# The last batch's second product transposed, two of its three column pairs by Strassen's scheme

## The chip, the cores and the metric

The kernel runs on one core of one Trainium2 chip. The metric is the device time of one execution in microseconds (us). A core has five engines with instruction streams of their own: PE (TensorE, matrix products; its weight loads are listed apart as PEld), DVE (VectorE), ACT (ScalarE), POOL (GpSimd) and SP (SyncE, which here only issues transfers). Data lie in DRAM, in the on-chip memory of 128 partitions (SBUF), and in the accumulators of TensorE (PSUM). Transfers are packets on 16 DMA engines, which one queue of SP feeds here; they are taken in the order of issue.

## The reference

Sigmoid attention for 8 batches of 12 heads (448 positions, 64 columns a head), and on its result, as rows of 768, a feed-forward product of 2048 hidden columns.

```python
def _attn_ref(q, k, v):                       # (8, 12, 448, 64)
    scores = q @ k^T / sqrt(64) - log(448)
    return (1 / (1 + exp(-scores))) @ v

def _moe_ref(x, w_in, w_out):                 # x (3584, 768), w_in (768, 2048), w_out (2048, 768)
    h = x @ w_in
    g = h - tanh(h)
    return g @ w_out                          # (3584, 768), float32
```

## The kernel before, in words

The work goes by batches of 448 rows. A batch has attention for six pairs of heads, the *first product* h = x w_in with g = h - tanh(h) as a polynomial behind it, and the *second product* out = g w_out. Each float32 product is made of float16 parts, a high and a low one, as three matmuls: high by high, high by low, low by high. Splitting a value takes one ACT operation (the high part) and one DVE operation (value minus high part). Batch 0 also streams the weights in and converts them; its order of work is a string of letters (`ORDER`), and the program's scheduler sets where its transfers stand in SP's queue. From batch 1 on the order in every engine's stream is that in which the code emits the instructions.

`Builder` is the general program and `Small(Builder)`, a subclass, the path that runs here; the general one stands behind a branch that is not taken.

The first product. Batches 0 to 2 make it classically. From batch `SEVEN` = 3 on it goes by a scheme of Strassen's kind: each of eight pairs of hidden column blocks (k = 0 to 7, each pair holding 256 of the 2048 hidden columns) is made with seven products of half size in place of eight. `seven` emits one, 9 matmuls of 224 columns; a pair has 63. The weights' sums for a pair form a *set* of 1344 KB, kept in DRAM. `fetch(n)` loads a set into one of three slots (`RING`), when `close(k)`, the last two products of the set that had the slot, has been issued. In `Small.moe1` a round of k is `front`, `copy`, `seed`, `cross`, `middle`, `reseed`, `close` (the products and the sums between them in PSUM), then `square`, `times`, `curve`, `value` (the polynomial, on ACT and DVE), and `highs` and `lows` (the split of g). These sets are made in batches 1 and 2 from the converted weights; the transfers `set<-wi` and `set<-unit` (L1267, L1309) store them.

The second product. `moe2` goes over three tiles of 128 tokens. For each it makes both halves of 384 output columns, 16 row tiles of w_out with three matmuls of 384 columns: 288 matmuls (`po`, L921). 64 tokens are left, `por`: 96 matmuls (L969) that fill half of the array each. While the second product of batch b runs, the attention of batch b+1 is done by ACT, DVE and POOL in pieces (`blocks`) between its steps. In the last batch no attention is left, so the second product stands alone, except that `FILL` = 2 of its steps (12 matmuls) are issued ahead of `close(7)`.

Batch 0's weights. w_out comes in 32 pieces `rawo` of 128 x 384 (32-bit words), 16 row tiles for each half of the columns. `conv_load` (L172) issues the load. The conversion turns the raw values into float16 parts in place and ends with `conv_end`. The parts of w_out stay in SBUF in `wo` for the whole program, those of w_in until batch 3 writes its ring over them.

Of the kernel before, what the change touches and what calls it, by code (L numbers as in the profile page):

```python
# [8 lines left out]
F16 = mybir.dt.float16  # L9
# [10 lines left out]
P = 128  # L20
D = 64
# [21 lines left out]
class Builder:  # L43

    KAPPA = KAPPA

    SUMS = 1.0
    NORMS = (3, 5, 7)

# [390 lines left out]
    def defers(self, g):  # L440
        return False

    def split_a(self, a, dve):
# [6 lines left out]
        nc.vector.scalar_tensor_tensor(A[:, 1], a[:, 0], A_SCALE, A[:, 0], op0=ALU.mult, op1=ALU.subtract)  # L450
        return A
# [54 lines left out]
    def stream(self):  # L506
# [120 lines left out]
        for g in range(0, G, 2):  # L627
            h = g + 1
            early = g == 0

            aa = units(g, (0, 1))
            do_av()
            if early:
# [48 lines left out]

            aa = units(h, (2,), lambda: parts_k(g + 3))
            if early:
                do_av()
            keep(h, (2,), aa)
            parts_q(g + 3)
# [102 lines left out]

    def g_scales(self, m):

# [12 lines left out]
        V.tensor_tensor(g2, hb, h3, op=ALU.min)  # L805
        V.tensor_scalar(g2, g2, 2.1, TINY, op0=ALU.mult, op1=ALU.max)
        y = self.pow2(g2, 1, "g")
# [35 lines left out]
    def moe1(self, b, st, splits, ahead):  # L843
# [7 lines left out]
        for k in range(self.NF // 2):  # L851
            ph = self.ps.tile([P, 2, 512], F32, name="ph", tag="sc", bufs=2)
            for e in range(2):
                if e < splits[k]:
                    next(self.rest, None)
                self.product(ph[:, e, :S], self.ks[k], e, xhl)
            g = self.gp.tile([P, 2, 2, S], F16, name="g", tag="g")
            self.gs.append(g)
# [42 lines left out]
    def moe2(self, b, gs):  # L901
# [10 lines left out]

        def store(o, j0, n, cols, queue=nc.sync):
            queue.dma_start(self.out[base + j0 : base + j0 + n, cols], o)

# [66 lines left out]


    def build(self):
        nc, tc = self.nc, self.tc
# [35 lines left out]
    def first(self, weights, early, late):  # L1021
# [13 lines left out]
        def room():  # L1035
            self.stage.release()
            self.gp = self.tc.alloc_tile_pool(name="gp", bufs=self.NF // 2, reuse_waits="tile")

        def mixture():
# [16 lines left out]
            if e:  # L1056
                g = self.gp.tile([P, 2, 2, S], F16, name="g", tag="g")
# [130 lines left out]
class Small(Builder):  # L1188
# [5 lines left out]
    SEVEN = 3  # L1194
    FILL = 2
    RIGHT = {1: 0, 2: 3, 3: 1, 4: 2, 5: 6, 6: 4, 7: 5}
    COPYFIRST = True
# [19 lines left out]
    def __init__(self, ctx, tc, flag, *args):  # L1217
# [13 lines left out]
        self.sets = kept("set", (self.NC // 2, 2, 7, P), F16)  # L1231
        self.raws = kept("raw", (self.NC, 256), F32)
        self.half = self.S // 2
        self.flat = self.wi.rearrange("p a b c -> p (a b c)")
        self.nextx = 0

    def ring(self, n):
# [110 lines left out]
    def high_on_dve(self, g, n, of):  # L1348
        return g >= (self.SEVEN - 1) * self.NP and ((n == 0 and of == 2 and self.HIGHS) or (of == 1 and self.HIGH1))

    def defers(self, g):
# [124 lines left out]
    def moe1(self, b, st, splits, ahead):  # L1476
# [5 lines left out]
        h = self.half  # L1482
        ix, bound = st
        base = (b - self.SEVEN) * self.NB
        self.late = []
# [23 lines left out]
        def copy(k):  # L1509
            copies[k] = c = self.tp.tile([P, 2, h], F32, name="cp", tag="t")  # L1510
            nc.scalar.activation(c[:, 0], banks[k][0][:, h:], AF.Copy)
# [44 lines left out]
        def value(k):  # L1556
            u, m = ms[k]
            V.scalar_tensor_tensor(m, u, C_S, m, op0=ALU.add, op1=ALU.mult)  # L1558

        def tail():  # L1560
# [10 lines left out]

        self.gs = [self.gp.tile([P, 2, 2, self.S], F16, name="g", tag="g") for _ in range(self.NB)]
        for k in range(2):
# [5 lines left out]
        ih, ihk = self.h_scales(ix)  # L1579
        self.Sg, self.iSg = self.g_scales(bound)  # L1580
        for k in range(2):
# [5 lines left out]
        for k in range(1, last):  # L1587
# [6 lines left out]
            seed(k + 1)  # L1594
            value(k - 1)
            close(k)
            square(k)
            times(k)
            m, g = ms[k - 1][1], self.gs[k - 1]
            self.highs(m, g)  # L1600
            cross(k + 1)
            middle(k + 1)
            self.lows(m, g, (0,))
            reseed(k + 1)
            self.lows(m, g, (1,))
            del ms[k - 1]
            if k in self.DEFER and b + 1 < self.B:
# [7 lines left out]
        self.tail = tail()  # L1615

# [81 lines left out]
```

## Time and profile before

| what | value |
|---|---|
| runs | 1139.45, 1138.1, 1138.54 us; median 1138.54 |
| profiled execution | 1139.2 us, span of the instructions 1137.3 us |
| granted TensorE clock | 1.000 of full speed |
| DMA queue of SP | 63696 packets, 147.55 MB, 38.0% of the 16 engines' time |
| last batch, first product | ends with the second product's first steps from 1075.9 us on |
| last batch, second product | 1079.6 to 1132.4 us |

A row of a group reads: line, engine, operation, output <- inputs, shapes, count, then busy us and the mean ns of one, then the idle time ahead of them and what ended it. A row of a timeline has the start in us, the duration in us, and the same names. In a row with "x2" behind it the duration runs from the first one's start to the last one's end. The chain lists, in order of time, the pieces of work that released one another up to the end.

### The profile page before, as it was taken

The numbers are of one execution on the slowest core, as the hardware profiler recorded it, in microseconds if no ns is written. First come the engines' busy times: TensorE is split into PE (matmuls) and PEld (weight loads), VectorE is DVE, ScalarE is ACT, GpSimd is POOL, SyncE is SP. The second block draws the span as 40 slices with busy tenths as digits, with TensorE's granted clock in tenths as the row PEclk, the third lists the DMA queues.
The fourth block names the chain that finished last, engine by engine and source line by source line (L and its number), as shares of the span: only waits on it lengthen the run. The fifth ranks groups of instructions, "written<-read, shape, count | busy, mean of one in ns | idle before, by whom it ended". The sixth has DMA issues, their size and how long they took to land.

```text
span 1137.3 us, 21304 instructions
## 1 busy us (share of the span) xinstructions
PE 1123.9 (99%) x8678; PEld 702.5 (62%) x8678; DVE 807.6 (71%) x1302; ACT 739.7 (65%) x1159; POOL 216.5 (19%) x229
## 2 busy tenths in 40 slices
PE   9999999999999999999999999999999999999998
PEld 2345444555555554569855796559955697559965
DVE  6989699676678787777767686786867777636710
ACT  7987786555886467775676667675676766644610
POOL 0033200014020485310034002320033100330000
PEclk9999999999999999999999999999999999999999
DMA  9992171353222447215622174224622156003301
GB/s 363 404 354 74 29 219 54 83 125 112 75 80 59 141 144 268 73 40 199 236 72 63 51 279 145 63 64 143 246 98 65 43 206 231 17 14 138 128 15 37
DMA packets 64023, 149.28 MB, mean 131 GB/s; under 512 B 18480, under 2 KB 41776, under 8 KB 58800
## 3 DMA queue, kind: packets, MB, share of 16 engines
q1 hardware_dynamic: 63696, 147.55, 38.0%
q8 instruction: 69, 1.13, 0.4%
q10 hardware_dynamic: 224, 0.33, 0.1%
q14 instruction: 34, 0.28, 0.1%
HBM read 119.54 MB, written 28.31 MB: 130 GB/s over the span
## 4 chain that ended last, share of the span: by engine, by line
PE 88%; DMA 4%; DVE 3%; ACT 2%; issue 1%; POOL 1%; SPq 0%; ACTq 0%; DVEq 0%; POOLq 0%
PE po L921 29%; PE ph L1467 16%; PE ph L835 9%; PE acc L463 8%; PE sc L423 8%; PE ph L1047 6%; PE por L969 6%; PE phq L1467 3%; PE php L1467 2%; DMA raw<-moe_w_in 2%; DVE wo L264 1%; ACT a L434 1%; DMA qnn<-q 1%; DVE wi L264 1%; DMA wi<-raw 1%
## 5 line engine op out<-in xcount | busy, mean ns | idle before, releaser
L921 PE MATMUL po<-wo,g 128*128 128x384 f16 x2304 | 389.5, 326 | 1.4 <-DVE g L829 0.7
L921 PEld LDWEIGHTS <-g 128*128 128x128 f16 x2304 | 220.5, 98 | 165.1 <-issue 24.3
L1467 PEld LDWEIGHTS <-wi 128*128 128x128 f16 x2520 | 241.2, 98 | 3.5 <-issue 2.4
L450 DVE SCALAR_TENSOR_TENSOR ahl<-a,ahl 128x896 f16<-128x896 f32 x126 | 156.5, 1254 | 61.7 <-ACT ahl L449 60.3
L434 ACT ACTIVATE a<-sc,nls,rn 128x896 f32<-128x896 f32 x147 | 156.3, 1094 | 50.9 <-PE sc L423 49.5
L1467 PE MATMUL ph<-wi 128*128 128x224 f16 x1890 | 188.5, 259 | 0.1
L494 POOL TENSOR_TENSOR x<-x 128x448 f32<-128x448 f32 x24 | 24.9, 1037 | 488.3 <-ACT x L477 488.3
L835 PE MATMUL ph<-xhl,wi 128*128 128x448 f16 x576 | 109.3, 352 | 0.0
L423 PE MATMUL sc<-Q,K 64*128 64x448 f16 x1008 | 100.8, 353 | 2.4 <-ACT a L434 2.4
L835 PEld LDWEIGHTS <-wi 128*128 128x128 f16 x576 | 56.2, 98 | 52.8 <-issue 0.6
L463 PE MATMUL acc<-ahl,vhl 128*64 128x448 f16 (+1 forms) x864 | 80.6, 356 | 0.0
L449 ACT ACTIVATE ahl<-a 128x896 f16<-128x896 f32 x85 | 79.3, 944 | 0.6
L1047 PE MATMUL ph<-x,wi 128*128 128x448 f32 x192 | 74.5, 541 | 0.0
L423 PEld LDWEIGHTS <-K 64*128 64x128 f16 x1008 | 35.6, 97 | 54.2 <-issue 32.9
L969 PE MATMUL por<-wo,g 128*64 128x384 f16 x768 | 64.9, 327 | 0.0
L463 PEld LDWEIGHTS <-vhl 128*64 128x64 f16 (+1 forms) x864 | 38.4, 108 | 40.2 <-issue 19.8
L1544 ACT ACTIVATE u<-ph,ih 128x896 f32<-128x896 f32 x30 | 30.3, 1009 | 43.7 <-PE ph L1467 43.7
L1047 PEld LDWEIGHTS ph<-x,wi 128*128 128x128 f32 x192 | 35.7, 190 | 33.1 <-issue 31.3
L969 PEld LDWEIGHTS <-g 128*64 128x64 f16 x768 | 42.4, 110 | 22.2 <-issue 4.5
L1458 DVE SCALAR_TENSOR_TENSOR g<-m,Sg,g 128x448 f16<-128x448 f32 x80 | 53.4, 678 | 3.7 <-ACT g L1452 3.7
L958 DVE TENSOR_SCALAR o<-po,iK 128x384 f32<-128x384 f32 x20 | 12.3, 616 | 58.9 <-PE po L921 43.5
L1452 ACT ACTIVATE g<-m,Sg 128x448 f16<-128x448 f32 x80 | 48.9, 660 | 6.9 <-DVE m L1558 5.8
(196 smaller groups left out, 1512.8 us busy)
## 6 DMA issues: line engine op xcount, KB each, us to landing
wi<-set SPq DMA_DIRECT2D x40, 1344.0 KB, 5.9
knn<-k SPq DMA_DIRECT2D x45, 224.0 KB, 2.6
qnn<-q SPq DMA_DIRECT2D x44, 224.0 KB, 2.7
rawo<-moe_w_out SPq DMA_DIRECT2D x22, 384.0 KB, 6.0
out<-o SPq DMA_DIRECT2D x21, 384.0 KB, 2.3
raw<-moe_w_in SPq DMA_DIRECT2D x13, 512.0 KB, 8.1
vn<-v SPq DMA_DIRECT2D x24, 256.0 KB, 3.0
raw<-wi SPq DMA_DIRECT2D x8, 768.0 KB, 8.0
```

The lines of the kernel that those rows point to most:

```text
L423: self.nc.tensor.matmul(ps[i * m : (i + 1) * m, h, : self.S], K[i][r, w, c * P : c * P + m], Q[i][r, x, :], start=(n == 0), stop=(n == len ...
L434: self.nc.scalar.activation(a[:, 0], ps[:, :, : self.S], AF.Sigmoid, bias=self.nls, scale=scale)
L449: nc.scalar.activation(A[:, 0], a[:, 0], AF.Copy, scale=A_SCALE)
L450: nc.vector.scalar_tensor_tensor(A[:, 1], a[:, 0], A_SCALE, A[:, 0], op0=ALU.mult, op1=ALU.subtract)
L463: self.nc.tensor.matmul(acc[i][h * D : (h + 1) * D, : self.S], v[k, w, 2 * QT + h if half else h * QT + c], A[k, x, h], start=(n == 0 and ...
L835: self.nc.tensor.matmul(ph, self.wi[:, self.slot(c, k), part, e * P : (e + 1) * P], xhl[c][:, x, :], start=(i == 0), stop=(i == len(prods) ...
L921: nc.tensor.matmul(po[i][:, :H], gs[f // 2][:, x, f % 2, tk * P : (tk + 1) * P], self.wo[:, i * self.NF + 2 * ks[f // 2] + f % 2, w], star ...
L969: nc.tensor.matmul(po[e * D : (e + 1) * D, :H], gs[f // 2][:, x, f % 2, nm:S], self.wo[:, e * self.NF + 2 * ks[f // 2] + f % 2, w], start= ...
L1047: nc.tensor.matmul(ph[:, e, :S], self.fp32(self.wi, self.slot(c, k))[:, 0, e * P : (e + 1) * P], xs[c], start=(c == 0), stop=(c == self.NC ...
L1452: self.nc.scalar.activation(high, src, AF.Copy, scale=self.Sg)
L1458: self.nc.vector.scalar_tensor_tensor(lows[i], srcs[i], self.Sg, highs[i], op0=ALU.mult, op1=ALU.subtract)
L1467: self.nc.tensor.matmul(out, w[:, c, part, left], self.xblock(c, x, right), start=start and i == 0, stop=i == len(prods) - 1, skip_group_c ...
```

## The change

Only the second product of batch 7 (`ACROSS` = 7) is replaced. It is made transposed: out^T = w_out^T g^T, with blocks of 128 output columns as the rows of a result and the 448 tokens as its columns. The rows of the last batch are written so, and the host puts them back when it gathers the output. The six blocks of 128 columns form three pairs, `PAIRS`. The pairs (0, 1) and (3, 4) are made by seven products of half size, whose weights are sums of w_out's blocks; the pair (2, 5) is made by eight products with the plain blocks. `across2` emits the products and `LAST7` writes out their order. `FILL7` = 4 steps (12 matmuls of 224 columns, the first of them 448) stand ahead of `close(7)` in place of `FILL` = 2.

What it adds besides:

- Batch 0. `conv_end` stores the raw values of the pairs' blocks in eight transfers of 512 KB to DRAM (`late<-wo`), one whenever four pieces of a half are complete.
- Batches 1, 3, 4, 5, 6. Sixteen *units* (`late_units`): two loads of raw blocks, four DVE additions on raw blocks, three of 128 columns and one of 256 (`late_add`), the split into high and low parts on ACT and DVE (`late_split`), two stores to DRAM (`lates<-lp`). `LATE` gives each batch's count in the first and the second product, and `STEPS`, `UNITS1` and `UNITS7` their steps.
- Batch 3. `plain_sets` copies w_out's kept parts of the third pair from SBUF to DRAM, eight transfers `lates<-wo` of 128 x 8 x 128 float16.
- Batch 7, first product. Each g is made in seven blocks of 224 columns, four of them sums or differences. `late_value` puts the polynomial's two halves into separate tiles (one of them `gq`, kept for the third pair), `late_sums` and `late_rest` form the sums on POOL (for k = 7 on DVE), and `late_parts` splits them, in DVE operations of 896 and 672 columns where two of 448 were. `late_fetch` loads the weights of the second product, 512 KB each, while the first product still runs: seven into the place where the other batches keep g, further ones into slots of the ring.
- The end. Each result tile of the third pair is scaled into 224 columns and stored by SP (`whole`), where a DVE operation of 384 columns and two stores, one on SP and one on ACT, stood.

SP's stream in batch 3, between the second product of batch 2 and the loads of the first product's sets. `out` are results, `set` a set in DRAM, `wi` the ring's place; the names with `late` are new. First before, then after:

```order
L914 DMA out<-o 128x768
L914 DMA out<-orem 64x384 x2
L1245 DMA wi<-set_112 128x5376
L1245 DMA wi<-set_113 128x5376
L1245 DMA wi<-set_114 128x5376
L1245 DMA wi<-set_115 128x5376
```

```order
L933 DMA out<-o 128x768
L933 DMA out<-orem 64x384 x2
L1397 DMA lates_135<-wo 128x8x128 x8
L1597 DMA wi<-set_112 128x5376
L1597 DMA wi<-set_113 128x5376
L1340 DMA wo<-late_126 128x2x128 x2
L1597 DMA wi<-set_114 128x5376
```

The eight copies now stand ahead of set 112, the fourth set that the first product of batch 3 uses (set 3 in the text), and the loads of a unit behind set 113.

SP's stream in batch 0, where the last pieces of w_out are loaded (`rawo`) among the loads of the next batch's attention inputs (`vn`, `knn`, `qnn`). First before, then after:

```order
L172 DMA rawo<-moe_w_out 128x384
L357 DMA vn<-v 128x512
L172 DMA rawo<-moe_w_out 128x384 x2
L347 DMA knn<-k 128x448
L172 DMA rawo<-moe_w_out 128x384
L347 DMA qnn<-q 128x448
L357 DMA vn<-v 128x384
L172 DMA rawo<-moe_w_out 128x384 x2
```

```order
L173 DMA rawo<-moe_w_out 128x384
L358 DMA vn<-v 128x512
L1308 DMA late_130<-wo 512x1x256
L173 DMA rawo<-moe_w_out 128x384 x2
L348 DMA knn<-k 128x448
L173 DMA rawo<-moe_w_out 128x384
L348 DMA qnn<-q 128x448
L358 DMA vn<-v 128x384
L173 DMA rawo<-moe_w_out 128x384 x2
```

One of the eight stores now stands ahead of the last five pieces.

DVE's stream in the first product of batch 7, one round (`ph` is PSUM, `cp` a copy of a part of it, `u` and `m` the polynomial's tiles, `gt` the sums; from here on `wo` is also the place of batch 7's g parts, whose home it takes). First before, then after:

```order
L1515 TENSOR_TENSOR ph<-ph,cp 128x224
L1558 SCALAR_TENSOR_TENSOR m<-u,m 128x896
L1550 SCALAR_TENSOR_TENSOR m<-ph,ihk,u 128x896
L1458 SCALAR_TENSOR_TENSOR g<-m,Sg,g 128x448
L1529 TENSOR_TENSOR ph<-cp,ph 128x448
L1458 SCALAR_TENSOR_TENSOR g<-m,Sg,g 128x2x224
```

```order
L1888 TENSOR_TENSOR ph<-ph,cp 128x224
L1455 SCALAR_TENSOR_TENSOR gq<-u,m 128x448
L1455 SCALAR_TENSOR_TENSOR m<-u,m 128x448
L1477 SCALAR_TENSOR_TENSOR wo<-m,Sg,wo 128x896
L1923 SCALAR_TENSOR_TENSOR m<-ph,ihk,u 128x896
L1902 TENSOR_TENSOR ph<-cp,ph 128x448
L1477 SCALAR_TENSOR_TENSOR wo<-gt,Sg,wo 128x672
```

The one operation of `value` became two, and the two splits of 448 became one of 896 ahead of `times` and one of 672 behind `reseed`.

The core of the diff:

```diff
+    PAIRS = ((0, 1), (3, 4), (2, 5))
+    LAST7 = (
+        "e04 T T T e03 e01 e14 e13 e11 e21 e23 m04 m03 m01 m14 m13 m11 m21 m23 l04 l03 c0 l14 l13 c1 Q "
...
+    FILL7 = 4
+    LATE = {1: (3, 0), 3: (1, 3), 4: (0, 3), 5: (0, 3), 6: (0, 3)}
...
+    def conv_end(self, p):
+        super().conv_end(p)
+        kind, r, i, n = p["piece"]
+        if kind == "out" and r % 4 == 3:
+            rows = self.fp32(self.wo, i * self.NF + r - 3, 4).rearrange("p f (b n) -> p f b n", n=P)
+            self.nc.sync.dma_start(self.late_raws[i][r // 4], rows[:, :, :2])
...
+    def late_add(self, u):
+        V = self.nc.vector
+        w = u[1][0]
+        V.tensor_tensor(w[:, 4], w[:, 0], w[:, 3], op=ALU.add)
+        V.tensor_tensor(w[:, 5], w[:, 2], w[:, 0], op=ALU.subtract)
+        V.tensor_tensor(w[:, 6], w[:, 1], w[:, 3], op=ALU.subtract)
+        V.tensor_tensor(w[:, 1:3], w[:, 1:3], w[:, 0:4:3], op=ALU.add)
+    def late_split(self, u):
+        raw, high, low = u[1]
+        self.nc.scalar.activation(high, raw, AF.Copy, scale=self.So)
+        self.nc.vector.scalar_tensor_tensor(low, raw, self.So, high, op0=ALU.mult, op1=ALU.subtract)
...
+    def plain_sets(self):
+        for n in range(4):
+            e, f = n % 2, n // 2
+            for x in range(2):
+                rows = self.wo[:, e * self.NF + f : (e + 1) * self.NF : 2, x, 2 * P :]
+                self.nc.sync.dma_start(self.late_sets[2][:, n, :, x], rows)
...
+    def late_sums(self, m, k, G):
+        h = self.half
+        t = self.tp.tile([P, 3, h], F32, name="gt", tag="t")
+        q, p = self.gq[k], m[:, 1]
+        G.tensor_tensor(t[:, 0], q[:, :h], p[:, h:], op=ALU.subtract)
+        G.tensor_tensor(t[:, 1], q[:, h:], p[:, :h], op=ALU.subtract)
+        G.tensor_tensor(t[:, 2], p[:, :h], p[:, h:], op=ALU.add)
+        return t
...
+            for k in ps:
+                for part, x in ((0, 0), (0, 1), (1, 0)):
+                    nc.tensor.matmul(
+                        p if wide == 2 else o,
+                        w[:, k, part],
+                        self.gq[k][:, x, right] if d == 2 and n > 4 else gs[k][:, x, right : right + wide],
...
+        if b == self.SEVEN:
+            self.plain_sets()
...
             seed(k + 1)
             value(k - 1)
+            m, g = ms[k - 1][1], self.gs[k - 1]
+            if late:
+                rest[k - 1] = m, self.late_sums(m, k - 1, nc.gpsimd), g
+                self.late_rest(m, k - 1, nc.gpsimd)
+                if k > 1:
+                    self.late_parts(*rest[k - 2], (1,))
             close(k)
...
-        self.ahead2 = self.moe2(b, self.gs)
-        for _ in range(self.FILL):
+        self.ahead2 = self.across2(b) if late else self.moe2(b, self.gs)
+        for _ in range(self.FILL7 if late else self.FILL):
             next(self.ahead2)
         close(last)
```

More of the change, by code (lines that the diff above doesn't have):

```diff
@@ L47 @@
     SUMS = 1.0
+    ACROSS = 7
     NORMS = (3, 5, 7)
@@ L1232, in __init__ @@
         self.raws = kept("raw", (self.NC, 256), F32)
+        self.marks = {}
+        self.late_raws = [
+            [self.drp.tile([P, 4, 2, P], F32, name=f"late{e}{i}", tag=f"late{e}{i}") for i in range(4)]
+            for e in range(2)
+        ]
+        self.late_sets = [
+            self.drp.tile([P, n, self.NB, 2, P], F16, name=f"lates{d}", tag=f"lates{d}") for d, n in enumerate((7, 7, 4))
+        ]
         self.half = self.S // 2
@@ new lines, in unit_plan @@
+    def unit_plan(self, b, which):
+        at = sum(sum(self.LATE[c]) for c in self.LATE if c < b) + sum(self.LATE[b][:which])
+        units = list(range(at, at + self.LATE[b][which]))
+        if b < self.SEVEN:
+            return units, ((1 if which else 3, 0),), 6 if which else 4
+        return units, ((0, 0), (1, 3)) if which else ((1, 0),)
+    def plain_sets(self):
[4 more added lines that the diff above has]
+                self.nc.sync.dma_start(self.late_sets[2][:, n, :, x], rows)
@@ new lines, in late_plan, with late_fetch @@
+    def late_plan(self):
+        self.late_at = {}
+        self.late_order = []
+        for b in range(self.ACROSS, self.B):
+            for word in (self.LAST7 if b + 1 == self.B else self.STEADY7).split():
+                if word[0] in "ew":
+                    d, n = int(word[1]), int(word[2])
+                    key = b, d, self.left_of(d, n)
+                    if key not in self.late_order:
+                        self.late_order.append(key)
+    def late_fetch(self, at):
+        if self.late_order:
+            b, d, i = self.late_order.pop(0)
+            self.late_at[b, d, i] = at
+            self.nc.sync.dma_start(self.late_ring(at), self.late_sets[d][:, i])
@@ L1237, in ring, with rows7, mm @@
+    def rows7(self, d):
+        return [slice(r * P, (r + 1) * P) for r in self.PAIRS[d]]
+    def mm(self, name):
+        return self.ps.tile([P, 512], F32, name=name, tag="mm", bufs=2)[:, : self.S]
     def ring(self, n):
@@ L1349, in high_on_dve, with beside, eager @@
         return g >= (self.SEVEN - 1) * self.NP and ((n == 0 and of == 2 and self.HIGHS) or (of == 1 and self.HIGH1))
+    def beside(self, b, k, e):
+        if b in self.LATE:
+            if k == e == 0:
+                if b == min(self.LATE):
+                    self.common_scale()
+                self.made = self.late_units(*self.unit_plan(b, 0))
+            for n in range(self.STEPS1[k]):
+                next(self.made, None)
+    def eager(self, g):
+        return g >= self.ACROSS * self.NP and g % self.NP == 0
     def defers(self, g):
@@ L1483, in moe1 @@
         ix, bound = st
+        late = b >= self.ACROSS
+        rest, fetches = {}, {}
+        if late:
+            if b == self.ACROSS:
+                self.late_plan()
+            fetches = {k: tuple(n for n in (2 * k - 2, 2 * k - 1) if n < 7 and b == self.ACROSS) for k in range(1, self.NB)}
+            if b + 1 == self.B:
+                fetches = {k: n + self.EXTRA7.get(k, ()) for k, n in fetches.items()}
         base = (b - self.SEVEN) * self.NB
@@ L1509, in copy @@
         def copy(k):
-            copies[k] = c = self.tp.tile([P, 2, h], F32, name="cp", tag="t")
+            pool, tag = (self.xp, "x") if late else (self.tp, "t")
+            copies[k] = c = pool.tile([P, 2, h], F32, name="cp", tag=tag)
             nc.scalar.activation(c[:, 0], banks[k][0][:, h:], AF.Copy)
@@ L1570, in tail @@
             self.late.append((ms[last][1], (self.gs[last],)))
-        self.gs = [self.gp.tile([P, 2, 2, self.S], F16, name="g", tag="g") for _ in range(self.NB)]
+        self.gs = [self.late_g(k) if late else self.gall[:, k] for k in range(self.NB)]
         for k in range(2):
@@ L1598, in moe1 @@
             times(k)
-            m, g = ms[k - 1][1], self.gs[k - 1]
-            self.highs(m, g)
+            if not late:
+                self.highs(m, g)
             cross(k + 1)
[L1602 to L1605, printed above, removed]
+            if late:
+                middle(k + 1)
+                reseed(k + 1)
+                if k > 1:
+                    self.late_parts(*rest.pop(k - 2), (0,))
+            else:
+                middle(k + 1)
+                self.lows(m, g, (0,))
+                reseed(k + 1)
+                self.lows(m, g, (1,))
             del ms[k - 1]
+            for n in fetches.get(k, ()):
+                self.late_fetch(n)
+            for n in range(self.STEPS[k]):
+                next(made, None)
             if k in self.DEFER and b + 1 < self.B:
@@ L1610, in moe1 @@
         value(last - 1)
-        self.ahead2 = self.moe2(b, self.gs)
-        for _ in range(self.FILL):
+        if late:
+            m, g = ms[last - 1][1], self.gs[last - 1]
+            rest[last - 1] = m, self.late_sums(m, last - 1, nc.gpsimd), g
+            self.late_rest(m, last - 1, nc.gpsimd)
+            self.late_parts(*rest.pop(last - 2), (0, 1))
+            self.late_parts(*rest[last - 1], (0,))
+        self.ahead2 = self.across2(b) if late else self.moe2(b, self.gs)
+        for _ in range(self.FILL7 if late else self.FILL):
             next(self.ahead2)
         close(last)
-        self.tail = tail()
+        for n in fetches.get(last, ()):
+            self.late_fetch(n)
+        for n in range(self.STEPS[last]):
+            next(made, None)
+        self.tail = late_tail() if late else tail()
     def products(self, b):
```

282 lines of the change are left out of this document (273 added, 9 removed), and 3 rows, old and new, of the table STEADY7.

## The prediction

> **What bounds the kernel now.** I read the page first: the busy shares, then the chain that ended last.
>
> ```profile
> PE 1123.9 (99%) x8678; PEld 702.5 (62%) x8678; DVE 807.6 (71%) x1302; ACT 739.7 (65%) x1159; POOL 216.5 (19%) x229
> ```
>
> ```profile
> PE 88%; DMA 4%; DVE 3%; ACT 2%; issue 1%; POOL 1%; SPq 0%; ACTq 0%; DVEq 0%; POOLq 0%
> ```
>
> TensorE is busy for 1123.9 of 1137.3 us, so time falls only where matmul time falls, and time is lost wherever the new work makes TensorE wait. The windows of the last batch come next (stretch; its length; busy us and count of PE, weight loads, DVE, ACT, POOL; granted clock; DMA share; GB/s), with two other places that I need below:
>
> ```profile
> 1028.00:1079.00 51.00, 50.98 (x525) 49.51 (x520) 33.46 (x59) 26.44 (x44) 0.00 (x0) 1.00 0.39 140
> 1079.00:1132.40 53.40, 53.35 (x379) 32.66 (x376) 6.73 (x12) 6.15 (x9) 0.00 (x0) 1.00 0.06 23
> 165.00:170.00 5.00, 5.00 (x38) 2.29 (x35) 4.31 (x8) 4.68 (x9) 1.14 (x1) 1.00 0.83 233
> 650.00:770.00 120.00, 120.00 (x1062) 82.67 (x1062) 88.30 (x135) 85.89 (x141) 21.66 (x23) 1.00 0.40 137
> ```
>
> In its first product (first row) and its second (second row) the last batch leaves TensorE no gap, at full clock, and in the second product everything else is nearly idle. The end of the chain (start, us, what) prices both products:
>
> ```profile
> 1067.28 8.62 PE ph L1467 x90
> 1075.90 1.95 PE po L921 x12
> 1077.85 1.73 PE ph L1467 x18
> 1079.58 44.85 PE po L921 x276
> 1124.43 7.94 PE por L969 x96
> 1132.37 0.02 issue
> 1132.39 0.62 DVE orem L978
> ```
>
> **1. The matmuls, the gain.** Before: 1.95 + 44.85 + 7.94 = 54.74 us for 288 matmuls of 384 columns and 96 in column halves. After: (7 + 7 + 8) products x 16 row tiles of w_out halved into 8 pairs x 3 parts = 22 x 24 = 528 matmuls of 224 columns, two of them twice as wide. A 224-column matmul of the same kind takes 8.62 / 90 = 0.0958 us; 528 of them and twice 0.093 for the extra width are 50.8 us, a gain of **-4.0 us**. The longer stretch gives 50.98 / 525 = 0.0971, which would make it 51.4 and -3.3; I take the chain's, because it has no 448-wide matmul in it, and keep -3.3 to -4.0.
>
> **2. The end.** The last evacuation is a DVE tile of 384 columns (0.62 us) now; then it is one of 224, about 0.40 (a 224-column row stands in part 5). The two last stores are issued side by side now, one by SP and one by ACT:
>
> ```profile
> 1133.04 0.48 SPq L914 DMA_DIRECT2D out<-orem  x1
> 1133.04 0.56 ACTq L914 DMA_DIRECT2D out<-orem  x1
> ```
>
> After the change both go through SP, the second 0.4 to 0.5 later, unless the first is already out by then. -0.22 + 0.45 = **+0.2** (-0.2 to +0.6).
>
> **3. Batch 3, the plain blocks.** Ahead of the load of set 3 in SP's queue come eight copies of 256 KB from the weights on chip to DRAM, in runs of 256 bytes, 8192 runs in all. The rows: SP's issues and the landing of one set (KB, us), then PE's use of that set; the last two are batch 1, where twelve transfers with the same 256-byte runs were issued, and the queue's packets, MB and share of 16 engines from 238 to 241 us.
>
> ```profile
> 510.34 1.11 SPq L914 DMA_DIRECT2D out<-orem  x2
> 518.53 0.34 SPq L1245 DMA_DIRECT2D wi<-set  x1
> ```
>
> ```profile
> wi<-set SPq DMA_DIRECT2D x1, 1344.0 KB, 5.8
> ```
>
> ```profile
> 524.56 1.89 PE L1467 MATMUL ph<-wi 128*128 128x224 f16 x18
> ```
>
> ```profile
> 234.61 6.15 SPq L1267 DMA_DIRECT2D set<-wi  x12
> ```
>
> ```profile
> q1 hardware_dynamic: 1571, 0.38, 57.0%
> ```
>
> Set 3 is issued at 518.53, when its slot comes free, lands 5.8 later at 524.4, and TensorE starts on it at 524.56: 0.2 us of slack. The copies can start at 511.45. 57% of 3 us on 16 engines is 27.4 us for 1571 packets, 17.4 ns for one; 8192 of them are 8.9 us of all sixteen engines. With some 1.5 us until the first moves (a small store takes 2.3 in all) they occupy the engines until about 522. Set 3 then begins behind them, with 1344 KB to move, and lands near 526.5: **+2.0**. Bounds: +0 if the copies drain before 518.5, +9 if SP's issue is what grows with the number of runs (rival B). Later sets are fetched as slots come free, all later by the same amount, so the loss is paid once. The Trainium skill, "DMA: Bandwidth & Descriptors", section "Anatomy of one DMA — SWDGE (gpsimd) path", fits a transfer as about 2.0 us plus its bytes at 436 GB/s and says that a DMA can emit many descriptors before they add cost; by that the 2.1 MB would be an estimated 6.8 us, over at 518.3, and the sum below would be 2.0 lower. The trace's 256-byte packets moved 0.38 MB in 3 us at a share of 57%, 222 GB/s at a full share, half that rate, so I take the trace.
>
> **4. Batch 0, the raw blocks kept.** Eight DMAs of 512 KB write w_out's columns 0-1 and 3-4 to DRAM while the weights stream in. The fourth (late_130) is ahead of the loads of pieces 11 to 15 in SP's queue. The chain there:
>
> ```profile
> 164.97 1.51 SPq L172
> 166.53 5.42 DMA rawo<-moe_w_out
> 172.24 0.27 issue
> 172.50 1.15 ACT wi L261
> ...
> 208.22 0.59 ACT oh L940
> 208.86 4.06 PE po L921 x24
> ```
>
> The load issued at 164.97 ends the chain's wait, and from it a chain of conversions on ACT and DVE runs to the matmuls at 208.86 without a pause. The queue moves 233 GB/s at a share of 0.83, 281 at a full one: 512 KB cost 0.524 / 281 = 1.87 us of it. With 17% of it free some of that is taken up: **+1.2** (0 to +1.9). The other seven stand at places where the queue's loads are not on this chain; nothing for them, and 1.9 for each that turns out to be.
>
> **5. Batch 7, first product.** Its g parts become seven blocks with sums, so VectorE's round changes. One round of before (start, us, engine, line, op, shapes, idle before):
>
> ```profile
> 1070.29 0.63 DVE L1529 TENSOR_TENSOR ph<-cp,ph 128x448 f32<-128x448 f32 x1 [0.51 <-ACT cp L1525]
> 1070.83 0.68 DVE L1458 SCALAR_TENSOR_TENSOR g<-m,Sg,g 128x448 f16<-128x448 f32 x1
> 1072.02 0.40 DVE L1515 TENSOR_TENSOR ph<-ph,cp 128x224 f32<-128x224 f32 x1 [0.51 <-ACT cp L1511]
> 1072.95 1.09 DVE L1558 SCALAR_TENSOR_TENSOR m<-u,m 128x896 f32<-128x896 f32 x1 [0.53 <-ACT u L1554]
> 1074.40 1.15 DVE L1550 SCALAR_TENSOR_TENSOR m<-ph,ihk,u 128x896 f32<-128x896 f32 x1 [0.36 <-ACT u L1544]
> 1075.46 0.68 DVE L1458 SCALAR_TENSOR_TENSOR g<-m,Sg,g 128x448 f16<-128x448 f32 x1
> ```
>
> That is 4.63 us in a round of 63 matmuls, 63 x 0.0958 = 6.04. The work on SBUF alone grows from 896 + 896 columns (1.09 + 0.68 + 0.68 = 2.45) to 448 + 448 + 896 + 672 = 2464: by the 1.09 row 3.0 us, by the 0.68 row 3.7, so about 3.4 and a round of 5.5. GpSimd gets three sums of 224 columns and one of 448 a round. What that does to VectorE shows where both work now:
>
> ```profile
> 718.50 3.65 DVE L450 SCALAR_TENSOR_TENSOR ahl<-a,ahl 128x896 f16<-128x896 f32 x2
> ```
>
> ```profile
> 719.34 1.87 POOL L503 TENSOR_TENSOR x<-x,x 128x448 f32<-128x448 f32 x1
> ```
>
> ```profile
> L1369 POOL TENSOR_TENSOR wi<-x,x 128x224 f32<-128x224 f32 x15 | 9.8, 655 | 37.1 <-ACT x L477 37.1
> ```
>
> Two VectorE operations of 896 columns took 3.65 us beside GpSimd, against 2 x 1.09: they wait for each other. GpSimd's 3 x 0.655 + 2 x 0.655 = 3.3 us (the 448 counted as two of 224) and VectorE's 3.4 together need 6.6 us of a 6.04 us round. If VectorE's operations on PSUM (2.2 us) can lie beside GpSimd, which no row here tells, the round is 0.6 too long in the worst order, and the slack in it (four waits of 0.36 to 0.53) is used up. At the product's end 18 matmuls (1.73 us, x18 in the chain) close the last block; ahead of them now stand 12 of 384 columns (1.95 us), then 12 of 224 (1.15). 0.8 us of cover goes where seeds are already tight. **+1.0** (0.2 to 3.4, the upper end 6 rounds x 0.56).
>
> **6. Batches 1 and 3 to 6, the 16 sums.** A unit is two loads, four additions, a split on ACT and one on DVE and two stores: by the 1.09 row some 2.2 us of DVE and 1.0 of ACT, three in a batch of 120. In the window 650 to 770 DVE is free for 31.7 us and ACT for 34.1, and TensorE has no gap, so 6.6 and 3.0 us are covered; what is not covered is a unit that stands ahead of an attention piece, up to 1.1 us at a time. **+0.3** (0 to +1.0). Without that cover all 16 would cost 35 us.
>
> **The sum**: -4.0 + 0.2 + 2.0 + 1.2 + 1.0 + 0.3 = +0.7 us. The profiled execution took 1139.2 us with a span of 1137.3, 0.7 over the median of 1138.54 (runs from 1138.1 to 1139.45), so 1139.9 in its terms and **1139.2 us** in the median's. What this measurement can tell from no change is 0.2%, 2.3 us: 1136.3 to 1140.8.
>
> **Rival A, faster.** The copies of part 3 are gone before set 3 is issued: at 281 GB/s, the full-share rate of the window from 165 us, 2.1 MB take 7.5 us, 511.45 to 519, about when set 3 is issued. Batch 0's slack in the queue takes late_130, and GpSimd finds its gaps. Then -4.0 + 0.2 + 0 + 0 + 0.5 + 0.3 = -3.0, **1135.5 us**. For it: TensorE's end is a clean 54.7 us of matmuls, and losses below 1.7 us in all are enough. Against it: 17.4 ns a packet, and 0.2 us of slack.
>
> **Rival B, slower.** SP itself takes long over 1024 runs: the twelve issues with 256 runs took 6.15 / 12 = 0.51 each, that of a set with 128 took 0.34. In proportion to runs eight issues of 1024 are 8 x 4 x 0.51 = 16.4 us, 511.45 to 527.9, and set 3, issued behind them, lands at 533.7: TensorE waits 9.1 us instead of 2.0, **1146.3 us**. It decides from 1.4 us an issue on (set 3 issued at 522.4, a stall of 3.6, a sum of 2.3). Against it: the two 64-run stores took 1.11 / 2 = 0.55 each, so the time of an issue does not follow the runs. By the difference of 0.34 and 0.51 alone, 0.17 for 128 runs, an issue of 1024 would be 1.5 and the stall near 4.7.
>
> **Rival C, slower.** VectorE and GpSimd exclude each other in every round of batch 7 (part 5's upper end): 3.4 instead of 1.0, **1141.6 us**. The four waits for ACT in the quoted round, 1.9 us, speak against it; 3.65 us for two operations speaks for it. The Trainium skill, "SBUF — State Buffer", section "SBUF: two separate sides", has this as an exclusive lock held for a whole instruction by whichever of a VectorE operation with two SBUF inputs and a GpSimd operation starts first; the 3.65 us agrees.
>
> That the change does not do what it says would show as more than 0.097 us a matmul; the 90 in a row of the same shape speak against it.
>
> **How the numbers follow.** The forecast, a stall of some 2 us at set 3 and a net near zero: 0.45. Rival A 0.25, B 0.17, C 0.13. The forecast's own range is 1137.6 to 1140.8. The range to 8 in 10 takes in A and C and leaves out most of B: 1135.3 to 1143.6. Faster by over 0.2%: most of A and a little of the forecast, 0.25. Within: 0.44. Slower: B, most of C and a little of the forecast, 0.31.
>
> **What would show it.** 528 matmuls near 0.096 us each at the end; a gap in PE ahead of its first use of set 3 (about 2 us; none for A, 5 or more with SP busy all the while for B); the conversions after the load of piece 11 about 1 us later against TensorE's first use of them; in batch 7 GpSimd's sums above 0.655 and VectorE's above 1.09 where they meet, and PE waiting for VectorE's seeds there. The prediction is wrong if there is a wait in batches 3 to 6 that I have put at nothing, or if the stores at the end are late.

## The result, and the profile after

The changed kernel takes 1146.29 us (median of 6 runs, 1144.17 to 1148.34), the kernel before 1138.99: ratio 1.0065, 95% interval 1.0052 to 1.0079. It is 7.3 us slower, outside the range. The profiled execution took 1148.34 us, 9.1 more than the one of before; the sums below go by these two, and the six runs of the changed kernel spread over 4 us where those of before spread over 1.5. Why they spread shows below.

The page's busy shares and chain, as shown of before:

```profile
PE 1125.1 (98%) x8822; PEld 720.9 (63%) x8822; DVE 871.3 (76%) x1413; ACT 762.8 (67%) x1186; POOL 249.4 (22%) x257
```

```profile
PE 68%; DVE 8%; DMA 4%; ACT 3%; issue 2%; SPq 1%; POOL 1%; DVEq 0%; POOLq 0%; ACTq 0%
```

TensorE is busy for 1125.1 us in place of 1123.9, though it has about 3 us less to do, and 7.9 us more of the span are idle. So two things are new: waits, and matmuls that take longer. The view of what TensorE waited for (total us, times, longest) names the waits; the list of before has neither the first, the third nor the fourth row:

```profile
PE ph L1831 <- DMA wi<-set: 5.0, 2, 3.7
PE sc L424 <- ACT a L435: 3.8, 4, 1.4
PE ph L850 <- DVE m L2087: 2.3, 1, 2.3
PE po L940 <- DVE o L977: 1.4, 4, 0.4
```

The matmuls up to the last second product are the same in both kernels, one by one, so the start of each can be subtracted from the start of its partner. That lag moves only at these places (us, the profiled executions):

| place | lag gained | of it idle | priced at |
|---|---|---|---|
| batch 0 and on, to 260 us | -0.3 | 0 | +1.2 (part 4) |
| batch 1, first product, 272.6 | +4.1 | 2.3 | in the +0.3 of part 6 |
| batch 2, to 500 us | -0.1 | 0 | 0 |
| batch 3, set 3, 528.4 | +5.2 | 3.7 | +2.0 (part 3) |
| batch 4, its first fetched set, 666.2 | +1.5 | 1.3 | 0 |
| batches 3 to 6, one evacuation each | +2.1 | 1.4 | in the +0.3 of part 6 |
| batch 7, first product | 0 | 0 | +1.0 (part 5) |
| last second product | -3.4 | 0.5 | -4.0 (part 1) |
| the end | 0.0 | | +0.2 (part 2) |

They add up to 9.1. In two places clearly more is lost than the wait. The windows of batch 1 (first three rows) and batch 3 (last four) show it (stretch; length; busy us and count of PE, weight loads, DVE, ACT, POOL; granted clock; DMA share; GB/s):

```profile
272.00:274.90 2.90, 0.62 (x4) 0.20 (x2) 2.59 (x4) 2.45 (x3) 1.04 (x2) 1.00 0.84 239
274.90:278.00 3.10, 3.08 (x10) 1.33 (x10) 3.08 (x3) 2.47 (x3) 3.10 (x3) 0.60 0.79 200
278.00:281.00 3.00, 3.00 (x15) 1.48 (x14) 2.95 (x4) 2.38 (x4) 1.75 (x3) 0.85 0.31 109
526.00:528.40 2.40, 2.40 (x26) 2.22 (x24) 2.11 (x3) 2.04 (x3) 0.00 (x0) 1.00 1.08 299
528.40:532.20 3.80, 0.07 (x1) 0.00 (x0) 2.53 (x4) 1.19 (x2) 0.00 (x0) 0.91 0.98 405
532.20:535.00 2.80, 2.79 (x16) 2.29 (x17) 0.00 (x0) 0.00 (x0) 0.00 (x0) 0.52 0.76 287
535.00:538.00 3.00, 3.00 (x34) 3.00 (x32) 1.58 (x3) 2.39 (x5) 0.00 (x0) 1.00 0.04 13
```

Behind the wait TensorE is busy all the time, but the granted clock is 0.52 to 0.60, and 16 matmuls take 2.8 us where 26 took 2.4. The "busy" column hides that loss. The same view, cut where the granted clock changes, shows where that happens (batch 1, then batch 3):

```profile
272.08:275.50 3.42, 1.12 (x7) 0.49 (x6) 3.11 (x4) 2.96 (x4) 1.64 (x3) 1.00 0.89 262
275.50:278.91 3.41, 3.41 (x11) 1.42 (x10) 3.38 (x4) 2.79 (x4) 3.41 (x3) 0.50 0.54 122
528.08:531.50 3.42, 0.40 (x5) 0.14 (x2) 2.85 (x5) 1.19 (x2) 0.00 (x0) 1.00 0.97 395
531.50:534.91 3.41, 2.70 (x15) 2.21 (x16) 0.00 (x0) 0.00 (x0) 0.00 (x0) 0.50 0.83 326
```

By the traces' record of the granted clock it changes in all ten profiled executions only at whole multiples of 3.41 us from one another; the two halvings above begin 256.0 us apart, 75 such stretches. A full clock was halved behind a stretch in which TensorE was busy for little (33% in the first row, 12% in the third, 37% at most over all executions), and never behind one with 52% or more. So what counts is not the length of a wait alone but how much of one stretch it fills, and half speed then lasts for whole stretches.

SP's stream in batch 3 answers to the rows of part 3 (start, us):

```profile
515.42 8.04 SPq L1397 DMA_DIRECT2D lates<-wo  x8
523.57 2.68 SPq L1597 DMA_DIRECT2D wi<-set  x2
```

The eight copies are issued in 8.04 us, 0.6 to 0.7 us each at first and 1.14 to 1.20 once the engines are full (their share is 1.06 to 1.10 from 518 to 526 us). The load of set 3 is issued at 523.57, where its slot had been free since about 522.2 (518.53 in the kernel before, and a lag of 3.7 by then), and lands 8.6 us later at 532.2, where 5.8 was usual. TensorE's rows:

```profile
527.45 1.03 PE L1831 MATMUL php<-wi 128*128 128x224 f16 x9
532.21 3.20 PE L1831 MATMUL ph<-wi 128*128 128x224 f16 x18 [3.73 <-DMA wi<-set]
535.24 1.89 PE L1831 MATMUL php<-wi 128*128 128x224 f16 x18
```

The middle row's 18 matmuls take 3.20 us, the last row's 1.89: half speed, then full.

In batch 1 the chain shows what was late (start, us, what):

```profile
262.96 0.52 SPq L1363
...
263.58 0.62 SPq L1363
...
264.25 0.74 SPq L1340
...
265.04 5.26 DMA lu<-late
...
270.39 0.29 DVE lu L1347
```

A unit's loads (L1340) are issued from 264.25 on, behind twelve transfers of the sets (in runs of 256 bytes) and the stores of the unit before (L1363), and the second lands 5.26 us after its issue at 265.04. VectorE has stood at the addition (L1347) all that time:

```profile
DVE lu L1347 <- DMA lu<-late: 5.5, 2, 5.3
```

Behind the additions, in VectorE's order, stand a split of the sets, the unit's split and the polynomial (`m`, L2087) that frees the accumulators for TensorE. VectorE was idle for 5.3 us and then everything came at once. The price of a unit was not its 2.2 us of work but the in-order wait for its load.

The evacuations of the second product (L977) were late by half a us once a batch, here in batch 3:

```profile
608.10 1.22 DVE L1347 TENSOR_TENSOR wi<-wi 128x128 f32<-128x128 f32 x1
609.24 0.74 DVE L1348 TENSOR_TENSOR wi<-wi 128x128 f32<-128x128 f32 x1
609.90 0.74 DVE L1349 TENSOR_TENSOR wi<-wi 128x128 f32<-128x128 f32 x1
610.68 0.76 DVE L1350 TENSOR_TENSOR wi<-wi 128x256 f32<-128x256 f32 x1
611.36 0.60 DVE L977 TENSOR_SCALAR o<-po,iK 128x384 f32<-128x384 f32 x1
```

Four additions take 3.3 us just ahead of it, where those of batch 1 took 0.28 to 0.43 each; GpSimd is at its sums of the next batch there, and the operations of the two engines start in turn, some 0.7 us apart on each:

```profile
609.12 0.71 POOL L1733 TENSOR_TENSOR wi<-x,x 128x224 f32<-128x224 f32 x1
609.79 0.70 POOL L1734 TENSOR_TENSOR wi<-x,x 128x224 f32<-128x224 f32 x1
```

The traces of the eight kernels with units hold 128 such groups of four additions. The 20 with GpSimd busy all through took 3.34 to 3.36 us from the first one's start to the last one's end; the other 108 took 1.14 to 1.16, all but one of them with GpSimd idle.

The last batch has neither wait nor slow matmuls. Its first product, with VectorE at 94% and GpSimd at 61%, and its second product:

```profile
1060.00:1090.00 30.00, 30.00 (x315) 29.88 (x313) 28.23 (x37) 21.80 (x33) 18.23 (x20) 1.00 0.89 339
1090.00:1141.00 51.00, 50.91 (x529) 50.38 (x527) 21.95 (x38) 15.00 (x22) 4.89 (x5) 1.00 0.27 96
```

### The profile page after: what moved, and what is told of

The parts are those of the page before. It is cut to its first block, busy times and chain, and to the rows that moved or that the text cites. A ratio compares the mean times of both kernels' runs of the same rounds, so it can differ in the third digit from the quotient of the medians.

```text
span 1146.4 us, 21959 instructions
## 1 busy us (share of the span) xinstructions
PE 1125.1 (98%) x8822; PEld 720.9 (63%) x8822; DVE 871.3 (76%) x1413; ACT 762.8 (67%) x1186; POOL 249.4 (22%) x257
## 3 DMA queue, kind: packets, MB, share of 16 engines
q8 instruction: 70, 1.15, 0.4%
## 4 chain that ended last, share of the span: by engine, by line
PE 68%; DVE 8%; DMA 4%; ACT 3%; issue 2%; SPq 1%; POOL 1%; DVEq 0%; POOLq 0%; ACTq 0%
PE po L940 23%; PE ph L1831 15%; PE acc L470 7%; PE sc L424 7%; PE ph L850 4%; PE por L988 4%; PE phq L1831 3%; PE php L1831 2%; DMA wi<-set 1%; PE poa L1511 1%; DVE wi L265 1%; DMA set<-wi 1%; DMA lu<-late 1%; PE pob L1511 1%; DVE wo L265 1%
## 5 line engine op out<-in xcount | busy, mean ns | idle before, releaser
L940 PE MATMUL po<-wo,g 128*128 128x384 f16 x2016 | 343.0, 326 | 2.8 <-DVE o L977 1.4
L940 PEld LDWEIGHTS <-g 128*128 128x128 f16 x2016 | 192.2, 98 | 148.8 <-issue 26.5
L457 DVE SCALAR_TENSOR_TENSOR ahl<-a,ahl 128x896 f16<-128x896 f32 x126 | 151.9, 1218 | 56.5 <-ACT ahl L456 54.9
L501 POOL TENSOR_TENSOR x<-x 128x448 f32<-128x448 f32 x24 | 27.6, 1152 | 487.1 <-ACT x L484 487.1
L988 PE MATMUL por<-wo,g 128*64 128x384 f16 x672 | 56.9, 327 | 0.0
L1084 PEld LDWEIGHTS ph<-x,wi 128*128 128x128 f32 x192 | 35.8, 190 | 33.1 <-issue 31.7
L1923 DVE SCALAR_TENSOR_TENSOR m<-ph,ihk,u 128x896 f32<-128x896 f32 x30 | 34.5, 1150 | 21.8 <-ACT u L1917 21.8
L988 PEld LDWEIGHTS <-g 128*64 128x64 f16 x672 | 37.1, 110 | 19.5 <-issue 4.2
L510 POOL TENSOR_TENSOR x<-x,x 128x448 f32<-128x448 f32 x21 | 35.7, 1702 | 45.1 <-ACT x L499 43.7
L1822 DVE SCALAR_TENSOR_TENSOR g<-m,Sg,g 128x448 f16<-128x448 f32 x64 | 42.7, 678 | 2.9 <-ACT g L1816 2.9
## 6 DMA issues: line engine op xcount, KB each, us to landing
vn<-v SPq DMA_DIRECT2D x24, 256.0 KB, 3.2
```

Of the source, the lines that this page charges most:

```text
L510: nc.gpsimd.tensor_tensor(out, self.x2, x2, op=ALU.add)
L940: nc.tensor.matmul(po[i][:, :H], gs[f // 2][:, x, f % 2, tk * P : (tk + 1) * P], self.wo[:, i * self.NF + 2 * ks[f // 2] + f % 2, w], star ...
L988: nc.tensor.matmul(po[e * D : (e + 1) * D, :H], gs[f // 2][:, x, f % 2, nm:S], self.wo[:, e * self.NF + 2 * ks[f // 2] + f % 2, w], start= ...
L1084: nc.tensor.matmul(ph[:, e, :S], self.fp32(self.wi, self.slot(c, k))[:, 0, e * P : (e + 1) * P], xs[c], start=(c == 0), stop=(c == self.NC ...
L1822: self.nc.vector.scalar_tensor_tensor(lows[i], srcs[i], self.Sg, highs[i], op0=ALU.mult, op1=ALU.subtract)
```

## The experiments

The theory: the loss has three places, the copies ahead of set 3, the additions in batch 1 that wait for their loads, and the additions ahead of evacuations; with the halved clock after the two long waits. The rival: the 16 units and the 27 MB more of transfers cost time wherever they stand.

**Copies moved.** The copies leave the place ahead of set 3 and are issued two a batch from the events of the second products of batches 3 to 6:

```diff
         if b == self.SEVEN:
-            self.plain_sets()
+            pass
...
+        if self.SEVEN <= b < self.ACROSS:
+            at = 2 * (b - self.SEVEN)
+            events += [(p, lambda i=i: self.plain_set(i)) for i, p in ((at, 13), (at + 1, 44)) if i >= 0]
```

> The changed kernel with the eight copies of the plain blocks taken from their place ahead of set 3 and issued two a batch in the second products of batches 3 to 6. Theory (a wait of 3.7 us for set 3 behind the copies, and about 1.3 us of matmuls at half speed after it): 5 us less than the changed kernel, near 1141.3, and no wait of PE for a set in batch 3. Rival (the copies cost their engine time wherever they stand, since other loads are then late): within 1.5 us of the changed kernel, near 1146, with new waits for loads in batches 3 to 6. Rival (SP's issue is what holds up, 1.2 us a copy): as the theory in time, but the copies' issues in the second products stay at 1.1 us or more each.

Measured: 1140.08 us, ratio to before 1.0007 (0.9998 to 1.0017), 6.2 us less than the changed kernel. No wait for a set is left in batch 3, and none came elsewhere for the copies. The theory's 5 us hold; the rest lies in batch 1, where this profiled execution lost 2.1 us and not 4.1 with the same code. Seven of the copies' eight issues took 0.43 to 0.67 us in their new places and one 1.40, so the second rival does not hold. One wait for a set is there, in batch 4:

```profile
PE ph L1830 <- DMA wi<-set: 1.7, 1, 1.7
```

It is the first set that batch 4 fetches, with 0.2 us of slack. It landed after 7.9 us here, 7.4 in the changed kernel, 7.2 and 7.7 in two more of the ten profiled executions and 5.6 to 5.8 in the other six; nothing else was in the queue. The same load took 5.5 to 5.8 us in batches 5 to 7 of all ten. What makes the one in batch 4 slow these runs don't show.

**Copies alone.** The kernel before with the eight copies at the same place:

```diff
+        if b == self.SEVEN:
+            for n in range(4):
+                e, f = n % 2, n // 2
+                for x in range(2):
+                    rows = self.wo[:, e * self.NF + f : (e + 1) * self.NF : 2, x, 2 * P :]
+                    self.nc.sync.dma_start(self.late_set[:, n, :, x], rows)
```

> The kernel before with the eight copies alone, at the place where the changed kernel has them (written to DRAM and never read). Theory: the copies by themselves make set 3 late, 3.7 us of wait and 1.3 of half speed, 1144 us. Rival (set 3 is late only together with the other work of the change, by my first price): 2 us, 1141.

Measured: 1144.31 us, ratio 1.0052 (1.0037 to 1.0066), 5.2 us over before. The view of TensorE's waits has one new row:

```profile
PE ph L1468 <- DMA wi<-set: 3.5, 1, 3.5
```

So the copies cost their 5 us with nothing else of the change present.

**How many copies fit.** Four, then six, of the eight ahead of set 3, the others in the second products (`i >= 4`, `i >= 6` in the events above, and `for i in range(4)` or `range(6)` where `plain_sets` stood).

> The changed kernel with four of the eight copies left ahead of set 3, the other four in the second products of batches 5 and 6. The copies drained 1.3 us apiece (10.4 us for eight). Theory (what matters is when the engines have drained the copies): four are gone at 521.5, before set 3's slot is free at 521.8, so no wait for set 3, and the time is that of the kernel with all copies later, 1140 us (1139 to 1141.5). Rival (anything in the queue ahead of set 3 makes it late in proportion): half of the loss, 1143.

> The same with six copies ahead. Theory: they drain at 524.1, set 3 lands at 529.5, where TensorE wants it at 528.5: a wait of about 1.0 us. If half speed follows only a longer idle time, as the waits of 0.5 to 0.7 us elsewhere and of 3.7 us here suggest, the loss is 1.0 and the time 1141.1; if half speed follows it too, 1142.3. Rival in proportion: three quarters of the loss, 1144.5.

Measured: 1141.65 us with four, 1141.88 with six, ratios 1.0022 (1.0012 to 1.0031) and 1.0019 (1.0010 to 1.0029). With four there is no wait for set 3 at all; the time is over the 1140 expected, and in the profiled execution batch 1 lost its full 4.2 us:

```profile
PE ph L850 <- DVE m L2090: 2.4, 1, 2.4
```

The granted clock is 0.998 or less in seven of these ten runs, the profiled one among them, and in two of the eleven with all copies later, which speaks for more halvings of the clock here.

With six, set 3 cost 0.5 us of lag (a wait of 0.4), less than the 1.0 expected, and no half speed. So four copies cost 0, six 0.5, eight 3.7 and the clock: not in proportion. From six to eight the engines' work grows by 2.6 us, but set 3 lands 10.0 us after its slot is free in place of 6.5. SP, held at the full queue, issued set 3 only 1.4 us after the slot was free; with six it issued it at once:

```profile
514.43 5.64 SPq L1396 DMA_DIRECT2D lates<-wo  x6
521.28 3.97 SPq L1596 DMA_DIRECT2D wi<-set  x2
```

That late issue left no gap on the engines: with eight copies the last one's packets end at 526.5, and the first packet of set 3 starts at 526.2. The copies end 4.3 us after the slot is free with eight and 2.0 with six. Besides, set 3 lands 5.6 us behind their end with eight and 4.5 with six; why, these runs don't show.

**Units spread in batch 1.** Two units in its first product and one in its second, with six half rounds a unit and the additions three half rounds behind their loads:

```diff
-    LATE = {1: (3, 0), 3: (1, 3), 4: (0, 3), 5: (0, 3), 6: (0, 3)}
+    LATE = {1: (2, 1), 3: (1, 3), 4: (0, 3), 5: (0, 3), 6: (0, 3)}
...
-            return units, ((1 if which else 3, 0),), 6 if which else 4
+            return units, ((3, 0),), 6
```

> The changed kernel with batch 1's three units spread: two in the first product, their additions three half rounds behind their loads in place of two, the third in the second product. Theory (VectorE stands at an addition whose load is not there, and the polynomial that TensorE waits for is behind it; 2.3 us of wait and 1.4 of half speed): 3.7 us less than the changed kernel, near 1142.6, and no wait of PE in batch 1's first product. Rival (batch 1 is short of VectorE time or of transfer time, whatever the order): 1 us less or nothing, 1145.3 to 1146.3, the wait moved to another round.

Measured: 1144.0 us, ratio 1.0048 (1.0033 to 1.0062), 2.3 less than the changed kernel. Batch 1's first product has no wait and loses nothing, in place of 4.1; the unit in its second product costs 0.6. The median fell by less than 3.7. In the profiled execution set 3, still behind the copies, cost more than in the changed kernel: behind its wait of 3.5 us 30 matmuls went at half speed, against 13 in the changed kernel and 17 with the copies alone.

```profile
528.87 3.54 PE L1831 MATMUL ph<-wi 128*128 128x224 f16 x18 [3.46 <-DMA wi<-set]
532.20 3.13 PE L1831 MATMUL php<-wi 128*128 128x224 f16 x18
535.17 2.08 PE L1831 MATMUL ph<-wi 128*128 128x224 f16 x20
```

So about the same wait costs 1.3 to 2.9 us behind it, by where it falls among the stretches of 3.41 us: here the clock stayed at half for two of them, with TensorE busy for 72% of the first, and in the changed kernel for one, with 79%. That is part of the spread between runs; of the changed kernel's six the fastest, 1144.17 us, has a granted clock of 1.000, the others 0.997 or 0.998.

**All three.** Copies moved, units spread in batch 1, and the steps of the third unit in the second products put behind the evacuation:

```diff
-    UNITS7 = (2, 5, 8, 11, 14, 17, 20, 23, 26, 29, 32, 35, 38)
+    UNITS7 = (2, 5, 8, 11, 14, 17, 20, 23, 26, 33, 34, 35, 38)
```

> Both of the above, and the unit steps of batches 3 to 6 that stand ahead of an evacuation of the second product moved behind it. Theory (the loss is these three places and TensorE's half speed after two of them): the matmul gain of 3.4 us is left, 1135.6 us (1135 to 1137), with no wait of PE above 0.7 us but those of the kernel before. Rival (the 16 units and 27 MB more of transfers cost time all over): 1139 or more.

Measured: 1141.15 us, ratio 1.0019 (1.0010 to 1.0029): a miss. The three waits are gone, and a new one is there:

```profile
PE acc L470 <- ACT tn L376: 5.0, 4, 1.5
```

1.5 us in each of batches 3, 4 and 5: behind the evacuation come the norms of the attention, and the unit's operations now stand ahead of those. 4.7 us were given back by a step moved past one deadline to the next. The third unit of a second product fits at neither of these two places.

**Two units a second product.** The unit that had no place goes to the first product of each batch, where batch 3's single unit had cost nothing, and to batch 1: first with two units in each product of batch 1, then with three and one and, in its first product, a cycle of five half rounds with the additions three behind the loads.

```diff
+    LATE = {1: (2, 2), 3: (1, 2), 4: (1, 2), 5: (1, 2), 6: (1, 2)}
```

```diff
+    LATE = {1: (3, 1), 3: (1, 2), 4: (1, 2), 5: (1, 2), 6: (1, 2)}
...
-                elif (h - at) % cycle == cycle // 2 and i in held:
+                elif (h - at) % cycle == 3 and i in held:
                     self.late_add(held[i])
-                elif (h - at) % cycle == cycle // 2 + 1 and i in held:
+                elif (h - at) % cycle == 4 and i in held:
                     self.late_split(held[i])
...
-            return units, ((1 if which else 3, 0),), 6 if which else 4
+            return units, ((3, 0),), 6 if which else 5
```

> All copies in the second products, and the 16 units placed anew: two in the first and two in the second product of batch 1 with the addition three half rounds behind its load, and one in the first and two in the second product of batches 3 to 6, so that no addition stands ahead of an evacuation or of an attention norm late in the second product. Theory (a unit costs only where its addition or split delays something that TensorE waits for): only the matmul gain of 3.4 us and up to 0.7 in batch 1 are left, 1136.3 us (1135.5 to 1137.3). Rival (each unit costs wherever it is): 1139 to 1141.

> As the one before, but with three units in the first product of batch 1 as in the changed kernel, a cycle of five half rounds and the addition three behind its load instead of two, and one in its second product. Theory (in batch 1 it was the addition's wait for its load, not VectorE's work): the same time as the one before within 0.5 us, near 1136.3, and no wait for the unit's load that delays TensorE in batch 1. Rival (three units are more than batch 1's first product can take): a wait of 2 us or more there, 1138.5 or above.

The first took 1141.94 us, ratio 1.0026 (1.0016 to 1.0036), a miss; the second **1136.32 us, ratio 0.9980 (0.9971 to 0.9990)**, faster than both kernels and at the 1136.3 expected, though 5.6 us from the first, where 0.5 had been expected. TensorE's waits in the second:

```profile
PE sc L424 <- ACT a L435: 3.2, 4, 1.5
PE warm L115 <- DVE nls L1025: 1.3, 1, 1.3
PE pbn L374 <- ACT sqn L366: 0.7, 1, 0.7
PE po L940 <- DVE g L844: 0.7, 1, 0.7
PE po L940 <- DVE wo L265: 0.6, 1, 0.6
PE acc L470 <- ACT tn L376: 0.5, 1, 0.5
```

They are those of the kernel before but for 0.2 us. The lag at the start of the last second product is 0.3, the end 3.1 us earlier than before. Batch 1 has three units in its first product again, as the changed kernel has; there they come every five half rounds in place of four, the additions and splits stand one half round later behind their loads, and VectorE no longer waits for a load. So in batch 1 it was the order and not the amount of work; the spacing and the delay were not run apart. The rival for the whole is out: this kernel has all 16 units, all copies and the same 27 MB.

The first lost 2.1 us in batch 1, where the second unit of the second product stands ahead of an evacuation, and 1.7 to a slow landing in batch 4:

```profile
PE po L940 <- ACT o L973: 1.0, 1, 1.0
PE po L940 <- DVE o L977: 0.9, 1, 0.9
```

Besides, its device time stands 4.5 to 5.9 us over its span in all nine runs, against 1.7 to 2.0 in every other kernel here. What lies around the span is not in the trace, so that part stays open.

## Why the prediction was wrong, point by point

**1. The matmuls**: right within its bounds. 528 matmuls start 0.096 us apart, with three gaps of 0.5 us in all between them; -3.4, between -3.3 and -4.0. The longer stretch, with such gaps in it, priced it better than the chain's 90 matmuls.

**2. The end**: +0.0 for +0.2. The two stores went through SP in 0.81 us, and still the last matmul is followed by 5.0 us of span in both kernels.

**3. The copies**: the mechanism was right, the size was not. The copies took 10.4 us of the sixteen engines where I had 8.9 (some 20 ns a packet for the 17.4 of the sample). The 6.8 us by the Trainium skill's formula in part 3 were further off. Set 3 landed 5.6 us behind the last of them, where I had taken 4.5; SP issued it 1.4 us late, but no engine stood idle for that. The wait was 3.7 for 2.0. The term that I did not have at all is the halved clock, 1.3 us behind the wait here and up to 2.9 in the other kernels. The sum was 5.2 for 2.0, inside the bound of 9. Rival B's number, 1146.3, was nearly met, but not by its mechanism: an issue took 0.6 us while the queue had room, though it had 1024 runs, and 1.2 only when it had none. That the totals meet is luck: the copies cost 5.2 us, and rival B had a stall of 9.1.

**4. Batch 0**: wrong by 1.2. The eight stores cost nothing that TensorE shows: its lag up to 190 us is -0.2. The loads of the last five pieces landed a median of 4.2 us after their issue, 4.1 before, so the queue, free for 17% of the time there, took the 512 KB in. That is the lower end of my range.

**5. Batch 7's first product**: wrong by 1.0. VectorE is busy for 28.2 of 30 us and GpSimd for 18.2, and TensorE has no gap: the round just fits. Rival C's loss did not come; the tail's chain through VectorE and GpSimd cost 0.3 us at one point of the second product. The twelve matmuls ahead of `close(7)` are all of 224 columns in the trace; the two of 448 come behind it.

**6. The units**: this step failed. +6.2 (4.1 and 2.1) for +0.3 with a bound of 1.0. I compared VectorE's work with its idle time in a batch, 6.6 us with 31.7. What counts is what stands behind a unit's instruction on its engine, and whether the load it needs is there. I did not look where SP would issue the loads: in batch 1 behind twelve transfers with 256-byte runs, the very rows that I had quoted for the copies. In the second products a row of GpSimd's sums beside VectorE, which I had quoted for batch 7, would have warned that additions there can take far longer: 3.3 us and not 1.2.

The Trainium skill, "TensorE: Matmul & The Clock Gate", section "HAM oscillation — how this bites in real kernels", warns of gaps in TensorE's work above some 3.4 us, after which the next matmuls run at half rate. The runs agree on the half rate (0.187 us a matmul for 0.096) and differ on the length: waits of 2.3 and 2.4 us in batch 1 were followed by it, waits of 1.0 to 1.7 us in these runs were not. By the rule, the 2 us that I expected would have cost nothing behind them. By the shares measured here no run decides it: a wait of 2 us within one stretch of 3.41 leaves TensorE busy for 41% of it, between the 37% that were followed by half speed and the 52% that were not.

What stays open is how much of the 7.3 us in the medians is the slow landing in batch 4, a wait that I had put at nothing. It is in four of the ten profiled executions, all of them with the units, but absent in five others that have units or copies.

## What to carry to other kernels

Work put into idle time costs what stands behind it in its engine's order, not its length: for each added instruction, name what it waits for, and the next thing on that engine that the bound engine needs. Transfers ahead of a load with 0.2 us of slack make it late by what has not drained when its place comes free, and a wait that fills most of one 3.41 us stretch is paid again at half speed. With the copies two a batch, the additions of batch 1 later behind their loads and one unit fewer in each second product of batches 3 to 6, the same change went from 1146.3 to 1136.3 us. A gain of 0.3% in a kernel whose main engine is busy for 99% has to be followed with the lag of each matmul against its partner, since the busy shares hide every one of these places.

## What was not expected of the hardware

- TensorE's clock was granted at half after waits of 2.3 us and more (matmuls of 224 columns 0.187 us apart for 13 to 30 of them, of 448 columns 0.373), and at full after 1.7 us and less. It changed only on a fixed grid of 3.41 us, from full to half behind stretches with TensorE busy for 37% or less, never behind 52% or more.
- An issue of a transfer with 1024 runs took SP 0.6 us with a free queue and 1.2 with a full one; the load behind them was then issued 1.4 us after it could have been, without an idle engine for it.
- 256-byte runs from SBUF to DRAM moved at about 210 GB/s with all sixteen engines busy (2.1 MB from 516.5 to 526.5 us), loads of a set at about 400 (the window from 528.4 us).
- Four short additions on VectorE took 3.3 us with GpSimd busy beside them and 1.15 without.
